# A linear recurrence and a soft mixture of experts on one core: wider slot-sum matmuls, and unread matmuls put at other places

## The chip, the cores and the metric

The kernel runs on one core of a Trainium2 chip. The metric is the device time of one execution in microseconds. Before the change it is 197.21 us, the median of three runs (196.96 to 197.81).

## The reference

Two layers, one after the other. The first is a gated recurrence over 5056 steps for 4 batches and 256 channels; the second is a soft mixture of 8 experts with 4 slots each, over all 20224 tokens.

```python
sig = 1.0 / (1.0 + np.exp(-f_logit))
f = lower_bound[None, None, :] + (1.0 - lower_bound[None, None, :]) * sig
i = 1.0 - f
for t in range(S):
    h = f[:, t] * h + i[:, t] * x[:, t]
    y[:, t] = h
...
logits = x @ phi                     # x is y, with batch and step as one axis
d = softmax(logits, over tokens)
slot_input = d.T @ x                 # 32 slots x 256
for e in range(E):                   # w1: 256 x 1024, w2: 1024 x 256 for each expert
    slot_out[e] = np.maximum(slot_input[e] @ w1[e], 0.0) @ w2[e]
c = softmax(logits, over slots)
out = c @ slot_out
```

## The kernel before, in words

The sequence is cut into groups of 512 steps (ten groups, the last one overlapping), and a unit is one group of one batch: 40 units, n = 0 to 39. SP's queue issues all loads of f_logit and x, in the order of the units, into three buffers each (`load`), so a load waits until an older buffer is free. Each unit then goes through a chain of engines, and the order of all instructions is written out by hand in the loop over n:

- `gate` (ACT) makes s_t, the sigmoid of minus f, two units at once; `enter` (POOL) multiplies it by x into u_t (unit 0 on DVE).
- `s_to_channels` and `u_to_channels` (TensorE) transpose s and u, so that channels lie on partitions. From unit 4 on u is transposed by `half_to_channels`, 64 rows at a time.
- `decay` (ACT) makes the decay factors a from the transposed s, and `scan` (DVE) runs the recurrence, two scans a unit.
- `to_tokens` (TensorE) transposes the result back into hp, and `keep_tokens` (DVE or ACT in turn) copies it to ht.
- `logits`, `exps` and `weights_to_tokens` make exp(logits) for a pair of groups in the order of slots (etall) and of tokens (et). `slots` adds up et.T @ ht in slot_ps: a matmul for each batch and each r of a group, with 32 columns of weights and 256 columns moving. Batch b's sums stand in partitions 32b and up, all in the first half of the bank slot_bank.

`idle` issues matmuls that nobody reads, into the second half of slot_bank, each with a 128x128 float32 operand held (ident_f) and 256 columns moving; the profile has two records for each. `spin` issues such matmuls in bfloat16 during the experts.

POOL also issues the weight loads (`load_w`): w1 of eight experts, then w2 of eight, three early ones at n = 9, 17 and 25 and the rest at n = 31 to 36, after the `enter` of that step. They convert float32 to bfloat16. The last two experts' w2 go to w_t, a reused f_t buffer, and the eighth expert's comes in three pieces.

After the last unit, the slot sums are copied to slot_sb by DVE, transposed into sin_ps (which lies in the bank `tail` together with the row sums), scaled to sin, and go through w1 (hi), a transpose, and w2: experts 0 to 3 into so4_ps, experts 4 to 7 into so_ps, one after the other (j = 0 to 3, eight matmuls each, line 696). DVE scales so_ps to slot_out. Only then the output can be made: matmuls of etall with slot_out (line 727) or slot_bd (lines 760 and 801), a scaling by DVE or ACT, and 20.7 MB of stores by SP. In the experts' stretch TensorE runs its instructions strictly in the order written.

Of the kernel before, what the change touches and what calls it, by code (L numbers as in the profile page):

```python
# [18 lines left out]
def kernel(  # L19
# [10 lines left out]
    nc = tc.nc  # L30
# [131 lines left out]
    with tc.tile_pool(name="sp2", bufs=3) as sp2, \  # L162
# [9 lines left out]
        slot_bank = pslot.tile([P, 2, D], F32, name="slot_ps")  # L172
        slot_ps = slot_bank[:, 0]

        wide_rep = rep.rearrange("p b s -> p (b s)").unsqueeze(1).broadcast_to([P, 2, P])

        def idle(k, first=False):
            if first:
                for i in range(2):
                    nc.tensor.matmul(slot_bank[:, 1, ds(0, P)], ident, ident,  # L180
                                     start=True, stop=False, skip_group_check=True)
            for _ in range(k):
                nc.tensor.matmul(slot_bank[:, 1], ident_f, wide_rep,  # L183
                                 start=False, stop=False, skip_group_check=True)
        xs, fs, sts, uts, pss, psus, hs, hps, hts, lgs, ets = ({} for _ in range(11))
# [73 lines left out]

        def half_to_channels(n, ps, t):  # L260
            k = ds(n % 2 * (P // 2), P // 2)
            v = ps.rearrange("c p r -> c (p r)").rearrange("c (p r) -> c p r", r=2 * R)
            for r in range(2 * R):
                nc.tensor.transpose(v[:, :, r], t(r)[k].bitcast(F32), ident_f[k, k])  # L264

# [9 lines left out]
        def u_to_channels(n):  # L275
            ps = psu.tile([P, P, R], F32, name="up", tag="up")
            if long(n):
                half_to_channels(n, ps, lambda r: uts[n - n % 2 + r // R][:, r % R])
# [139 lines left out]
        def left_over():  # L418
            for b in range(B):
                k = ds(b * NS, NS)  # L420
                nc.gpsimd.tensor_copy(left[k, :, b % 2], etall[k, ds(S - L, L)])

        def slots(g):
            n_p = rows(g)
            et, ht = ets.pop(g), hts.pop(g)
            for r in range(R):
                for b in range(B):
                    nc.tensor.matmul(slot_ps[ds(b * NS, NS), :], et[:n_p, r, b],
                                     ht[:n_p, b, r],
                                     start=(g == 0 and r == 0),  # L430
                                     stop=(g == n_grp - 1 and r == R - 1),
                                     skip_group_check=True)

# [36 lines left out]
        def late_slots():  # L470
            for r in range(R):
                for b in range(B):
                    nc.tensor.matmul(slot_ps[ds(b * NS, NS), :], ets[last][:, r, b],
                                     hts[last][:, b, r],
                                     start=False, stop=r == R - 1,
                                     skip_group_check=True)
# [6 lines left out]
        load(SINGLE)  # L483
        lb_constants()
        gate(0, 1)
        enter(0)
        s_to_channels(0)
        decay(0, 1, [0])
        u_to_channels(0)
        gate(1, 1)  # L490
        decay(0, 1, [1])
        phi_constants()
        enter(1)
        s_to_channels(1)
        u_to_channels(1)
        gate(2, 1)
        decay(1, 1)
        enter(2)
        for n in range(n_unit):
            if n < SINGLE - 2:  # L500
# [7 lines left out]
                if n + 3 == SINGLE:  # L508
                    gate(n + 3)
                if n % 2 == 0:  # L510
                    unit(load, n + AHEAD)
                unit(enter, n + 3)
                for b in range(2 * n, 2 * n + 2):
                    rep_constants(b)
            else:
                end = n >= n_unit - 6
# [30 lines left out]
                if n == n_unit - 2:  # L547
                    keep_tokens(n - 1)
                if n % 2 == 0:
                    unit(s_to_channels, n + 2)  # L550
                    unit(s_to_channels, n + 3)
                if n not in (n_unit - 3, n_unit - 2):
                    unit(u_to_channels, n + 1)
                if n in (n_unit - 5, n_unit - 4):
                    idle(2)
                elif n == SINGLE - 2:
                    idle(1, True)
                elif 2 * B <= n < n_unit - 4 and n % (2 * B) in (1, 5, 6, 7):
# [55 lines left out]
        slot_sb = slot_sb.rearrange("p t o -> p (t o)").bitcast(F32)[:, ds(0, D)]  # L614
        nc.vector.tensor_copy(slot_sb, slot_ps)
        sin_ps = tail[:, 0, ds(G // 2, DC * NS)].rearrange("p (o s) -> p o s", o=DC)
        slot_v = slot_sb.rearrange("p (c o) -> p o c", o=DC)
# [6 lines left out]
    with tc.tile_pool(name="ew", bufs=1) as ew, \  # L624
# [68 lines left out]
        nc.vector.reciprocal(rrow[:, :wide_r], rs_ps[:, :wide_r])  # L693
        for j in range(Q):
            for fc in range(FC):
                nc.tensor.matmul(so_ps, wide[:, fc, j].rearrange("p b s -> p (b s)"),
# [11 lines left out]
        nc.vector.tensor_scalar_mul(slot_out, so_ps, rcs)  # L708
# [161 lines left out]
```

## Time and profile before

| what | us |
|---|---|
| median of three runs | 197.21 |
| the profiled execution, whole | 197.01 |
| its span, first to last instruction | 195.2 |
| busy: TensorE, DVE, ACT, POOL | 150.6, 142.0, 138.8, 103.1 |
| first load issued; first f_t used by ACT | 0.72; 4.39 |
| first scan starts; last scan ends | 7.84; 125.6 |
| last weight issue; last weights landed | 126.92; 141.5 |
| first store issued | 143.58 |
| last instruction of the output stage on DVE and ACT | about 176.5 |

The scans of unit 0 start at 7.84 and those of unit 39 end at 125.6; in 110 to 120 us DVE is busy 10.00 of 10 us. Loads of x and f run until about 107 us, the weights until 141.5, the stores from 144 until about 193. The granted clock of TensorE is 0.50 in three stretches of 3.41 us, from 18.52, 35.59 and 49.24, and from 144.8 to the end; elsewhere the records show 1.00, and for the time before 15 us there is no record of it.

An idle time in a row, [0.27 <-DMA w_t], is the time the engine stood before the row's first instruction, with what ended it. PEld is the load of the held operand, PE the matmul itself; loads run ahead of matmuls.

### The profile page before, as it was taken

To read this page: it belongs to the slowest core of one execution; us is meant where nothing else is said; L and a number is where in the kernel's file an instruction comes from. 1 tells how busy PE (TensorE), PEld (TensorE's weight loads), DVE (VectorE), ACT (ScalarE), POOL (GpSimd) and SP (SyncE) were. 2 spreads that over 40 slices of the span, in tenths; PEclk is the share of its full clock that TensorE was granted. 3 is DMA by queue.
4 is the path that set the end of the run, shared out by engine and by line. 5 is a ranking of instruction groups with operands and counts; after the bars stand their busy time and mean duration, and the time that the engine had idled before them with its cause. 6 is when DMAs were issued, how large, how long until landed. Compare 5 with 4: busy or idle time off the path is not lost.

```text
span 195.2 us, 3283 instructions
## 1 busy us (share of the span) xinstructions
PE 150.6 (77%) x1222; PEld 108.7 (56%) x1222; DVE 142.0 (73%) x175; ACT 138.8 (71%) x192; POOL 103.1 (53%) x78
## 2 busy tenths in 40 slices
PE   0684896898998979989798976999997999980000
PEld 0474775765786657857576755766872663420000
DVE  2666699799699999999999999824288867770000
ACT  3686778599988998989988698724068788991000
POOL 2584888756798949776888979592030000000000
PEclk9998799699699999999999999999985555555555
DMA  6999999999999999999999999999949999999995
GB/s 203 415 433 428 426 425 421 430 426 411 326 428 426 423 334 405 423 425 414 324 418 418 235 212 214 214 212 211 170 165 428 425 431 426 430 433 430 430 430 218
DMA packets 12145, 70.75 MB, mean 362 GB/s; under 512 B 1361, under 2 KB 1874, under 8 KB 7650
## 3 DMA queue, kind: packets, MB, share of 16 engines
q1 hardware_dynamic: 9504, 62.13, 76.3%
q0 software_dynamic: 2624, 8.42, 21.8%
q8 instruction: 9, 0.15, 0.3%
q14 instruction: 6, 0.05, 0.1%
q10 hardware_dynamic: 2, 0.00, 0.0%
HBM read 58.23 MB, written 20.71 MB: 404 GB/s over the span
## 4 chain that ended last, share of the span: by engine, by line
PE 36%; DVE 28%; DMA 17%; ACT 4%; issue 4%; SPq 1%; POOL 0%; ACTq 0%
DVE h L332 17%; DMA w_t<-in_moe_w_dram 7%; PE op L801 7%; PE sp L249 7%; PE op L727 6%; DMA w_sb<-in_moe_w_dram 6%; PE hp L345 5%; DVE ht L364 5%; PE up L264 4%; DMA f_t<-in_f_logit_dram 4%; DVE h L319 3%; DVE oc L717 2%; PE op L760 2%; ACT s_t L234 1%; PE lg L378 1%
## 5 line engine op out<-in xcount | busy, mean ns | idle before, releaser
L245 POOL TENSOR_TENSOR u_t<-s_t,x_t 128x1024 bf16<-128x1024 bf16 (+1 forms) x39 | 82.4, 2129 | 24.5 <-ACT s_t L234 14.2
L332 DVE TENSOR_TENSOR_SCAN h<-a,h,up 128x512 bf16<-128x512 f32 x64 | 78.1, 1267 | 9.0 <-PE up L264 4.3
L234 ACT ACTIVATE s_t<-f_t 128x2048 bf16<-128x2048 f32 (+2 forms) x22 | 38.1, 1736 | 2.9 <-DMA f_t<-in_f_logit_dram 2.9
L345 PE MATMUL hp<-ident_f,h 128*128 128x128 f32 (+1 forms) x160 | 29.3, 307 | 8.4 <-DVE ht L364 6.3
L297 ACT ACTIVATE a<-sp,lbs 128x1024 f32<-128x1024 bf16 x28 | 29.6, 1112 | 4.6 <-PE sp L249 4.5
L345 PEld LDWEIGHTS hp<-ident_f,h 128*128 128x128 f32 (+1 forms) x160 | 23.2, 206 | 17.0 <-DVE ht L364 11.5
L249 PE MATMUL sp<-ident_f,s_t 128*128 128x128 f32 x144 | 23.7, 315 | 7.0 <-ACT s_t L234 5.7
L249 PEld LDWEIGHTS sp<-ident_f,s_t 128*128 128x128 f32 x144 | 19.6, 164 | 8.7 <-ACT s_t L234 6.5
L264 PE MATMUL up<-ident_f,u_t 64*128 64x64 f32 x224 | 21.4, 236 | 2.4 <-POOL u_t L245 2.4
L264 PEld LDWEIGHTS up<-ident_f,u_t 64*128 64x128 f32 x224 | 17.0, 144 | 7.1 <-POOL u_t L245 2.8
L721 ACT ACTIVATE ob<-op,rrow 128x256 f32<-128x256 f32 x32 | 12.4, 478 | 9.1 <-PE op L727 8.7
L364 ACT COPY ht<-hp 128x512 f32<-128x512 f32 (+1 forms) x21 | 12.2, 583 | 7.9 <-PE hp L345 7.9
L304 ACT ACTIVATE a<-sp,lbs 128x512 f32<-128x512 bf16 (+2 forms) x16 | 13.2, 868 | 2.9 <-PE sp L249 2.7
L183 PE MATMUL slot_ps<-rep,ident_f 128*128 128x256 f32 x42 | 14.2, 426 | 0.0
L364 DVE COPY ht<-hp 128x512 f32<-128x512 f32 (+1 forms) x19 | 12.7, 668 | 1.0 <-PE hp L345 1.0
L801 PE MATMUL op<-slot_bd,etall 64*128 64x512 bf16 x32 | 13.1, 627 | 0.0
L812 ACT ACTIVATE oc<-op,rrow 128x256 f32<-128x256 f32 x32 | 12.2, 486 | 0.8 <-PE op L801 0.3
L727 PE MATMUL op<-slot_out,etall 32*128 32x256 bf16 x64 | 12.6, 375 | 0.1
L806 DVE TENSOR_TENSOR oc<-op,rrow 128x1024 f32<-128x1024 f32 x8 | 9.7, 1223 | 3.4 <-PE op L801 3.4
L717 DVE TENSOR_TENSOR ob<-op,rrow 128x1024 f32<-128x1024 f32 (+2 forms) x12 | 9.8, 862 | 2.2 <-DMA out_dram<-ob 1.1
L727 PEld LDWEIGHTS <-etall 32*128 32x128 bf16 x64 | 8.9, 153 | 3.8 <-issue 1.3
L378 PE MATMUL lg<-h,phi 128*32 128x512 bf16 (+1 forms) x80 | 9.9, 389 | 0.2 <-ACT et L402 0.2
(109 smaller groups left out, 168.9 us busy)
## 6 DMA issues: line engine op xcount, KB each, us to landing
f_t<-in_f_logit_dram SPq DMA_DIRECT2D x14, 1024.0 KB, 11.2
x_t<-in_x_dram SPq DMA_DIRECT2D x14, 1024.0 KB, 9.5
out_dram<-oc SPq DMA_DIRECT2D x4, 2048.0 KB, 13.1
w_sb<-in_moe_w_dram POOLq DMA_DIRECT2D x14, 512.0 KB, 9.5
out_dram<-ob SPq DMA_DIRECT2D x3, 2048.0 KB, 9.6
f_t<-in_f_logit_dram SPq DMA_DIRECT2D x8, 512.0 KB, 7.0
x_t<-in_x_dram SPq DMA_DIRECT2D x8, 512.0 KB, 6.1
out_dram<-oc SPq DMA_DIRECT2D x4, 896.0 KB, 6.0
```

The lines of the kernel that those rows point to most:

```text
L183: nc.tensor.matmul(slot_bank[:, 1], ident_f, wide_rep, start=False, stop=False, skip_group_check=True)
L234: nc.scalar.activation(s_t, f_t, ACT.Sigmoid, scale=-1.0)
L245: nc.gpsimd.tensor_tensor(uts[n][:, :r], s_t[:, :r], x_t[:, :r], ALU.mult)
L249: nc.tensor.transpose(ps[:, :, r], t[:, r].bitcast(F32), ident_f)
L264: nc.tensor.transpose(v[:, :, r], t(r)[k].bitcast(F32), ident_f[k, k])
L297: nc.scalar.activation(a, sp[:, :, :, :, o], ACT.Identity, scale=nomlb[:, ds(o, 1)], bias=1.0)
L332: nc.vector.tensor_tensor_scan(h[:, :T, o], decays[n // 2, o][:, n % 2, :T], up[:, :T, o], hs[number(g - 1, b)][:, ds(used(g - 1) - 1, 1), ...
L345: nc.tensor.transpose(hp[:n_p, r], hw[:, :n_p, r], ident_f)
L364: copy(hts[g][:n_p, b].rearrange("p r d -> p (r d)").bitcast(F32), hps.pop(n)[:n_p].rearrange("p r c -> p (r c)"))
L717: nc.vector.tensor_tensor(ob, op, scale.broadcast_to(list(ob.shape)), ALU.mult)
L727: nc.tensor.matmul(op[:, j], ew[:, :, r + j], slot_out[ds(b * NS, NS)], start=True, stop=True, skip_group_check=True)
L801: nc.tensor.matmul(op[:, i_r].rearrange("p u d -> p (u d)"), ew[:, :, r + i_r], slot_bd[ds(j * 2 * NS, 2 * NS)].rearrange("s u d -> s (u d)"),
```

## The change

- `idle` no longer holds ident_f but zeros: the tile `left`, cleared at the start and filled only at the end, read as 64 float32 columns. So it adds zero to the sums of batches 0 and 1, and holds 64 columns in place of 128. What moves is ident_f repeated (`plain`) or rep.
- There are 36 such matmuls in place of 21: ten among units 0 to 3, one each at n = 2, 3, 5 and 7, and two within the transposes of unit 12; 20 stay where they were. The two bfloat16 ones that opened the bank go.
- The gate of units 4 and 5 is issued as two halves, and POOL's last two rep constants come before `enter` of unit 4, not after.
- `slots` of groups 0 to 5 takes two batches in one matmul: 64 columns of weights, 512 columns moving, 8 matmuls a group in place of 16. Only the blocks of a batch with itself are read, so sums of odd batches now stand in the second half of the bank (`slot_of`). The other groups still take 16.
- The slot sums are copied in four pieces, two by DVE and two by ACT, and sin_ps gets a bank of its own.
- Six spins of 512 columns stand before expert 6 (j == 2), and two of 512 behind the last expert in place of eight of 128.

```diff
-        slot_ps = slot_bank[:, 0]
+        zeros = left.rearrange("s t u -> s (t u)").bitcast(F32)
...
-        def idle(k, first=False):
-            if first:
-                for i in range(2):
-                    nc.tensor.matmul(slot_bank[:, 1, ds(0, P)], ident, ident,
-                                     start=True, stop=False, skip_group_check=True)
-            for _ in range(k):
-                nc.tensor.matmul(slot_bank[:, 1], ident_f, wide_rep,
-                                 start=False, stop=False, skip_group_check=True)
+        plain = ident_f.unsqueeze(1).broadcast_to([P, 2, P])
+
+        def idle(k, first=False, moving=wide_rep):
+            for i in range(k):
+                nc.tensor.matmul(slot_bank[ds(0, L), 0], zeros, moving,
+                                 start=first and i == 0, stop=False, skip_group_check=True)
...
-        def half_to_channels(n, ps, t):
+        def half_to_channels(n, ps, t, rests=False):
...
             for r in range(2 * R):
+                if r == R and rests:
+                    idle(2)
...
+        PAIRED = 6
+
+        def slot_of(b):
+            return slot_bank[ds(b * NS, NS), b % 2]
+
         def slots(g):
...
             for r in range(R):
+                if g < PAIRED:
+                    for b in range(0, B, 2):
+                        nc.tensor.matmul(slot_bank[ds(b * NS, 2 * NS)],
+                                         et[:n_p, r, ds(b, 2)].rearrange("p b s -> p (b s)"),
+                                         ht[:n_p, ds(b, 2), r],
+                                         start=(g == 0 and r == 0), stop=False,
+                                         skip_group_check=True)
+                    continue
                 for b in range(B):
-                    nc.tensor.matmul(slot_ps[ds(b * NS, NS), :], et[:n_p, r, b],
-                                     ht[:n_p, b, r],
-                                     start=(g == 0 and r == 0),
-                                     stop=(g == n_grp - 1 and r == R - 1),
-                                     skip_group_check=True)
+                    nc.tensor.matmul(slot_of(b), et[:n_p, r, b], ht[:n_p, b, r],
+                                     start=False, stop=False, skip_group_check=True)
...
         lb_constants()
+        idle(3, True, plain)
         gate(0, 1)
...
         u_to_channels(0)
+        idle(2, moving=plain)
         gate(1, 1)
...
         s_to_channels(1)
+        idle(1, moving=plain)
         u_to_channels(1)
...
                 if n + 3 == SINGLE:
-                    gate(n + 3)
+                    gate(n + 3, 1)
+                    gate(n + 4, 1)
                 if n % 2 == 0:
                     unit(load, n + AHEAD)
-                unit(enter, n + 3)
+                if n == 0:
+                    unit(enter, n + 3)
                 for b in range(2 * n, 2 * n + 2):
                     rep_constants(b)
+                if n:
+                    unit(enter, n + 3)
...
+                if n == SINGLE - 2:
+                    idle(4, moving=plain)
                 if n % 2 == 0:
                     unit(s_to_channels, n + 2)
...
-                elif n == SINGLE - 2:
-                    idle(1, True)
+                elif n in (SINGLE - 2, SINGLE - 1, SINGLE + 1, SINGLE + 3):
+                    idle(1)
...
-        nc.vector.tensor_copy(slot_sb, slot_ps)
-        sin_ps = tail[:, 0, ds(G // 2, DC * NS)].rearrange("p (o s) -> p o s", o=DC)
+        for b in range(B):
+            copy = nc.scalar.copy if b % 2 else nc.vector.tensor_copy
+            copy(slot_sb[ds(b * NS, NS)], slot_of(b))
+        sin_ps = psu.tile([P, DC, NS], F32, name="sin_ps", tag="up")
...
         for j in range(Q):
+            if j == 2:
+                spin(tail[:, 1], 6, G)
             for fc in range(FC):
...
-        spin(tail[:, 1], 8, P)
+        spin(tail[:, 1], 2, G)
```

More of the change, by code (lines that the diff above doesn't have):

```diff
@@ L277, in u_to_channels @@
             if long(n):
-                half_to_channels(n, ps, lambda r: uts[n - n % 2 + r // R][:, r % R])
+                half_to_channels(n, ps, lambda r: uts[n - n % 2 + r // R][:, r % R],
+                                 n == 3 * B)
             elif n // B == odd:
@@ L472, in late_slots @@
                 for b in range(B):
-                    nc.tensor.matmul(slot_ps[ds(b * NS, NS), :], ets[last][:, r, b],
+                    nc.tensor.matmul(slot_of(b), ets[last][:, r, b],
                                      hts[last][:, b, r],
```

## The prediction

> **What bounds the kernel now.** I read the slices of the page first, because they show which resource has no holes.
>
> ```profile
> PEclk9998799699699999999999999999985555555555
> DMA  6999999999999999999999999999949999999995
> GB/s 203 415 433 428 426 425 421 430 426 411 326 428 426 423 334 405 423 425 414 324 418 418 235 212 214 214 212 211 170 165 428 425 431 426 430 433 430 430 430 218
> HBM read 58.23 MB, written 20.71 MB: 404 GB/s over the span
> ```
>
> Every engine has slices of 8 or less; the DMA row has only 9s between its first slice and slice 30. The 212 GB/s of slices 23 to 28 is no slack: weights are read as float32 and stored as bfloat16, so 212 moved is 424 read. Next, stretches of 2 us around the one hole (columns: stretch, length, busy PE, PEld, DVE, ACT, POOL, then clock, DMA share, GB/s):
>
> ```profile
> 138.00:140.00 2.00, 2.00 (x23) 1.78 (x22) 0.76 (x2) 0.00 (x0) 0.00 (x0) 1.00 1.09 191
> 140.00:142.00 2.00, 1.73 (x18) 1.32 (x17) 0.02 (x1) 0.00 (x0) 0.00 (x0) 1.00 0.45 76
> 142.00:144.00 2.00, 1.87 (x21) 1.70 (x19) 1.58 (x5) 0.96 (x3) 1.36 (x2) 1.00 0.00 0
> 144.00:146.00 2.00, 1.96 (x10) 1.11 (x10) 2.00 (x4) 2.00 (x7) 0.47 (x1) 0.70 0.82 313
> ```
>
> Then the chain that ended last, where it crosses that hole:
>
> ```profile
> 115.00 11.64 DMA w_sb<-in_moe_w_dram
> 126.64 0.28 issue
> 126.92 14.59 DMA w_t<-in_moe_w_dram
> 141.52 0.04 issue
> 141.56 0.39 PE so_ps L696 x2
> 141.95 0.02 issue
> 141.98 0.49 DVE slot_out L708
> ```
>
> So the span of 195.2 is: about 2.6 us until the reads run at full rate; reads of 58.23 MB until the last weights land at 141.5 (419 GB/s over these 139 us); about 2.9 us without DMA while the last two expert matmuls, slot_out and the first output rows are made; 20.71 MB of writes until the DMA share falls at about 192.8 (428 GB/s); and some 2.4 us of closing. The profiled execution took 197.01, 1.81 more than its span; the median of the runs shown is 197.21 (196.96 to 197.81), so it stands 0.2 under the median.
>
> No byte, no DMA issue and no order within SP's queue changes. The change can move the end only through the hole: by when the last weights land, or by when TensorE has done the last expert.
>
> **How much room TensorE has there.** The timeline of TensorE and of its loads at the hole:
>
> ```profile
> 139.50 1.79 PE L696 MATMUL so_ps<-w_t,wide 128*128 128x256 bf16 x14
> 141.56 0.38 PE L696 MATMUL so_ps<-w_t,wide 128*128 128x256 bf16 x2 [0.27 <-DMA w_t<-in_moe_w_dram]
> 141.56 0.10 PEld L696 LDWEIGHTS <-wide 128*128 128x128 bf16 x1 [0.44 <-issue]
> ```
>
> The load for the last two matmuls stood 0.44 us: TensorE is only 0.44 us ahead of the last weights. Work put before that point costs what exceeds 0.44, unless TensorE arrives earlier. Call X the time by which it reaches j == 2 (139.50) earlier than before.
>
> **The parts.**
>
> Unread matmuls before the seventh expert (j == 2): six of 512 columns. None of that size at full clock is in the trace. Fourteen of 256 columns start over 1.79 less one of 0.27, 0.117 each, so 512 would take 0.23; by the old spins (eight of 128 columns in 0.61, 0.076 each) 0.30. At half clock, 32 op matmuls of 512 columns (L801) took 13.07, 0.41 each. Bounds 1.3 to 2.5 for six; I take 1.4, since the clock is 1.00 there. The delay of the last expert is then 1.4 - 0.44 - X, or 0.96 - X, never below nothing. The two spins left behind the experts (0.47) take the place of 0.61 and run beside slot_out's 0.49: nothing; uncovered, 0.47.
>
> Slot sums copied in four pieces, and sin_ps in a bank of its own: one DVE copy (0.42) becomes two on DVE and two on ACT, each priced by the whole copy or by ACT's 0.48 for 256 columns, so +0.42 to +0.54. Against it, DVE's sin waited 1.49 for row sums of the same bank, ending 131.21 though the sums' transposes were done at 130.46; that wait goes. The row sums stay in TensorE's queue ahead of the experts, so they begin about where they did: 0 (-0.5 to +0.3).
>
> First units. The largest idle time of DVE in the scans is here, and two more follow:
>
> ```profile
> 21.44 2.46 DVE L332 TENSOR_TENSOR_SCAN h<-a,h,up 128x512 bf16<-128x512 f32 x2 [2.63 <-PE up L249]
> 39.11 2.45 DVE L332 TENSOR_TENSOR_SCAN h<-a,h,up 128x512 bf16<-128x512 f32 x2 [1.51 <-PE up L264]
> 52.80 2.45 DVE L332 TENSOR_TENSOR_SCAN h<-a,h,up 128x512 bf16<-128x512 f32 x2 [1.61 <-PE up L264]
> ```
>
> All three stand behind TensorE at half clock (0.50 in 18.52 to 21.94, 35.59 to 39.00 and 49.24 to 52.66). At 21.44 the path was: gate of two units (1.91, to 18.47), eight transposes in 1.97, four in 0.8. Split, the first gate ends near 17.6, the second near 18.7 (1.06 each); at full clock the last four transposes of s take 0.63 and u's 0.63, so the scan starts near 20.05: +1.4 (0.5 to 1.8; the four unread matmuls end before 18.6 and so hold s back by up to 1 us). Rep constants moved past enter on POOL, two of 0.31, cost nothing: POOL would wait for the gate there anyway. The gap at 52.80 is met by two unread matmuls and by heavier slot sums in the stretch before it: +1.6 (0 to 1.6). The one at 39.11 gets one or two more matmuls in a stretch with 1.85 of 3.41 us busy: +0.5 (0 to 1.5). In the very first units three unread matmuls start after lb_ps at 3.55; at the half clock by which an old pair took 0.91 (21.47) they end near 6.2, and s_t is ready at 5.50; if they bring the clock up by 8.3 it is won back: 0 (-1.3 to +0.6).
>
> Slot sums of six groups: 16 matmuls of 32x256 took 0.62; now 8 of 64x512. The nearest row is the logits, 8 of 512 columns at two places of the array in turn, 1.08. So +0.46 a group, 2.8 us of TensorE in all (0 to 7.3, by 8 x 0.23 each). Half of it hides beside the scans; where DVE waits for u (0.39 at 55.64, 0.38 at 101.07) it shows. I take -1.0 (0 to -2.8).
>
> Unread matmuls of half the columns, 20 of them at the old places: their effect on the clock. I compared windows of 3.41 us that ended in a drop with those that didn't:
>
> ```profile
> 45.83:49.24 3.41, 2.44 (x30) 1.62 (x30) 3.41 (x5) 3.38 (x3) 1.22 (x1) 1.00 1.03 390
> 69.72:73.14 3.42, 2.45 (x30) 1.65 (x30) 3.42 (x5) 3.42 (x4) 2.26 (x2) 1.00 1.04 313
> 103.86:107.27 3.41, 2.59 (x19) 1.88 (x18) 3.41 (x5) 2.82 (x3) 3.39 (x3) 1.00 1.03 422
> 152.00:174.00 22.00, 22.00 (x76) 11.46 (x75) 16.90 (x15) 19.29 (x51) 0.00 (x0) 0.50 1.02 429
> ```
>
> The first dropped, the next two didn't, at equal busy time; and 22 us of full busy time with 32 or 64 rows stayed at half clock. Weighting each matmul's streaming time by its rows times columns over 128x128, I get 0.40, 0.41 and 0.41 for the first three: the clock seems to follow how much of the array is used, with a threshold near 0.4. By that estimate a half-wide unread matmul counts half, and 103.86 would fall to about 0.35. One such late drop costs DVE what the old ones did, about 1.5. I take half a drop: -0.8 (0 to -3). The Trainium skill, "TensorE: Matmul & The Clock Gate" ("The HAM clock gate"), says that the clock falls after an idle window of some 3.4 us. The trace agrees with the 3.41 us steps, but not that the window must be idle: 45.83 to 49.24 was 2.44 busy. By the skill's rule the narrower matmuls would cost nothing and X would be 0.8 larger.
>
> Sum: X = 1.4 + 1.6 + 0.5 + 0 - 1.0 - 0.8 + 0 = 1.7. That is above 0.96, so TensorE reaches the last weights before they land (141.5), and the hole is as before. What X exceeds 0.96 by is lost in waiting for weights: they can't land earlier, as the DMA share before them is 0.98 or more. So 197.01 + 0, or 197.2 against the median; I write 197.1.
>
> **Rivals.**
>
> 1. Slower: TensorE late at the seventh expert. If the clock drops after about 57 us (two or three drops at 1.5) or the slot sums cost 2.8, X is -0.5 to -1.5, and the six unread matmuls, which no wait hides any more, push the last expert by 0.96 + 0.5 to 1.5: 198.5 to 199.5. It decides from X = 0, where the time is 198.0. For it: scans keep DVE busy 10.0 of 10 us from 110 on, so nothing is won back there. Against it: DVE was idle 9 us in its first 50.
>
> 2. Faster: an earlier start fills the queues better and the last weights land sooner. From 140.00 to 141.25 the DMA share fell from 0.99 to 0.35; filled, that saves 0.4, and issues of POOL no longer held by a late scan might save as much again: 196.2. Against it: the last issues waited for earlier weight DMAs, not for POOL's work.
>
> 3. The change doesn't keep the clock up in the first units (half-wide again): X about -1, the same path as rival 1, with DVE's three gaps still there: 199.0.
>
> **Numbers.** No change to the end 0.70, rival 1 and 3 together 0.19, rival 2 0.11. A difference of 0.5% is 0.99 us, about what a measurement of this kernel can tell. The forecast's own range is 196.5 to 198.0 (X from 0 up, and the spread of runs); the low end stretches to 196.3 for rival 2 and the high end to 198.5 for the near part of rival 1. Rivals 1 and 3 make up slower, rival 2 faster.
>
> **What would show it.** Right: the last w_t lands at 141.5 within 0.5, the two last so_ps matmuls still start on that landing, DVE ends its scans 1 to 3 us before 125.6, no DVE wait over 1.5 in 18 to 54. Wrong: spins that end after w_t has landed, half-clock windows between 57 and 125, or a DMA share under 0.9 before 140. If weights land before 140.5, the claim that DMA bounds the first part is false.

## The result, and the profile after

The change made the kernel slower: 199.56 us, the median of six runs (199.16 to 200.78), against 197.23 for six runs of the kernel before (196.96 to 197.81). The ratio is 1.0127, with an interval of 1.0106 to 1.0149. The forecast of no change, 197.1 within 196.5 to 198.0, was wrong. The profiled execution took 199.62, its span is 197.8 (195.2 before). Runs of one kernel differ in their mean granted clock (0.857 to 0.879 in these six), and a ratio leaves out runs far above the fastest, so a median and a ratio need not agree.

The slices of the page after:

```profile
PEclk9999879999999999999999999999999555555555
DMA  5999999999999999999999999999529999999995
GB/s 209 418 432 427 427 421 427 429 426 381 356 426 421 414 328 429 421 430 368 363 417 381 203 210 214 215 212 211 97 108 433 422 421 444 444 434 424 424 424 215
HBM read 58.23 MB, written 20.71 MB: 399 GB/s over the span
```

The clock row has one dent where it had three. The unread matmuls help, but not in every execution alike: up to the first slot sums at 47 us the runs e1, e3, e6, e7, e8 and e10 below have the same instructions, and at half clock they spend there two, no, two, one, two and one steps of 3.41 us (two to four in the kernel before and its variants e4, e5, e9, e13 and e14). The bytes are the same. But the one hole of the DMA row, a 4 in one slice before, is now a 5 and a 2. The same stretches of 2 us as before (stretch, length, busy PE, PEld, DVE, ACT, POOL, then clock, DMA share, GB/s):

```profile
140.00:142.00 2.00, 1.95 (x13) 1.16 (x12) 0.71 (x2) 0.00 (x0) 0.00 (x0) 1.00 0.55 85
142.00:144.00 2.00, 2.00 (x18) 1.66 (x17) 0.00 (x0) 0.00 (x0) 0.00 (x0) 1.00 0.01 2
144.00:146.00 2.00, 1.85 (x15) 1.46 (x14) 1.58 (x5) 0.94 (x3) 1.34 (x2) 1.00 0.04 8
146.00:148.00 2.00, 1.96 (x12) 1.16 (x11) 2.00 (x4) 2.00 (x7) 0.49 (x1) 1.00 0.51 188
```

The DMAs stand still from 142 to 146, twice as long as before, and TensorE is busy all that time. The chain of waits names the work:

```profile
129.82 0.42 DVE slot_sb L637
130.24 0.02 issue
130.26 0.37 ACT slot_sb L637
130.64 0.02 issue
130.66 0.43 DVE slot_sb L637
131.09 0.02 issue
131.12 0.37 ACT slot_sb L637
...
139.91 0.89 PE so_ps L720 x8
140.81 0.33 PE tail L152
141.14 0.05 issue
141.19 1.02 PE tail L152 x4
142.22 1.76 PE so_ps L720 x16
143.98 0.02 issue
144.00 0.50 DVE slot_out L732
```

Where a DMA of w_t stood before, there is now an unbroken chain of TensorE's own work: TensorE reaches j == 2 at 140.81 (139.50 before), spins for 1.41 and runs the last 16 matmuls without a wait. They end at 143.98 (141.95), and the first store is issued at 145.61 (143.58): 2.03 later. The four copies stand in the chain one behind the other, 1.67 us from 129.82 to 131.49; one copy of 0.42 stood there before.

The other 0.57 lies behind the first store. From its issue to the last packet of the stores it takes 50.54 us, 49.97 before. What differs is seen among the packets of the trace, not among the instructions. The page's third part counts them on a queue of their own (packets, MB, share):

```profile
q8 instruction: 9, 0.15, 0.3%
```

These are 16 KB packets that fetch instructions, mostly 0.9 to 1.0 us each, on average one for every 250 of TensorE's records (100 to 330 in these two executions), and the page before has the same line. That they belong to TensorE is seen below, where added matmuls bring a tenth. What matters is the place of the ninth: 141.2 before, in the hole, and 145.6 now, at the issue of the first store, where it took 1.27 us and the second store's issue took 1.17 us in place of 0.38.

This table, from the packets and the instructions of each profiled execution, is used from here on (us; "records" are TensorE's matmul and load records):

```
run                               records  last fetches          last w_t  1st store  store stage  span
before                               2480  135.3  141.2            141.18     143.58       49.97  195.2
after                                2439  139.1  145.6            142.33     145.61       50.54  197.8
e1_no_spins_at_j2                    2440  140.5  147.4            144.56     146.93       50.71  199.3
e2_two_copies                        2448  138.8  147.1            144.67     147.00       50.75  199.4
e3_single_batch_sums                 2536  130.3  138.7  169.2     142.10     144.44       51.05  197.1
e4_spins_alone                       2480  134.8  140.9            141.06     143.95       49.97  195.6
e5_small_ones_before                 2536  131.5  139.3  169.1     142.04     144.39       51.00  197.0
e6_small_ones_after                  2479  137.7  143.0            143.30     146.70       49.96  198.3
e7_small_and_no_spins                2480  136.2  142.0            141.93     144.31       49.97  195.9
e8_two_groups_single                 2471  139.6  143.9            143.78     146.21       49.96  197.8
e9_weights_earlier                   2480  139.9  143.7            143.54     145.93       49.97  197.6
e10_first_units_only                 2536  131.5  138.6  169.3     142.22     144.62       50.90  197.1
e11_first_units_fewer_instructions   2464  133.1  142.7            141.21     143.59       49.96  195.2
e12_spins_with_early_scans           2463  137.8  142.0            141.23     144.45       49.96  196.1
e13_small_ones_at_the_end            2536  135.4  142.5  179.3     142.47     144.80       51.01  197.4
e14_eight_at_the_start               2496  133.5  141.2            141.51     143.86       49.96  195.5
```

"Last w_t" is the end of the last packet of the weights; the semaphore that TensorE waits for comes some 0.3 later, at the 141.5 of the table of before. "1st store" is its issue. First store, store stage and some 1.65 of closing make up the span of every row. In the three runs whose ninth fetch falls on the first stores (after, e1, e2) the second store's issue took 1.17, 1.35 and 1.38, and the store stage is 50.54 to 50.75.

### The profile page after: what moved, and what is told of

Same layout as the page of the kernel before. It is cut to its first block, busy times and chain, and to the rows that moved or that the text cites. A ratio compares the mean times of both kernels' runs of the same rounds, so it can differ in the third digit from the quotient of the medians.

```text
span 197.8 us, 3246 instructions
## 1 busy us (share of the span) xinstructions
PE 156.9 (79%) x1201; PEld 105.2 (53%) x1202; DVE 142.5 (72%) x176; ACT 139.7 (71%) x195; POOL 103.0 (52%) x78
## 4 chain that ended last, share of the span: by engine, by line
PE 34%; DVE 23%; ACT 12%; DMA 12%; POOL 4%; issue 4%; SPq 1%; ACTq 0%; POOLq 0%; DVEq 0%
DVE h L333 13%; DMA x_t<-in_x_dram 9%; PE op L825 7%; PE hp L346 5%; PE up L264 4%; POOL u_t L243 4%; PE sp L247 4%; DVE h L320 4%; DMA out_dram<-ob 3%; DVE ht L365 3%; ACT oc L791 2%; PE lg L379 2%; ACT s_t L232 2%; PE so_ps L720 2%; ACT a L298 2%
## 5 line engine op out<-in xcount | busy, mean ns | idle before, releaser
L346 PE MATMUL hp<-ident_f,h 128*128 128x128 f32 (+1 forms) x160 | 29.8, 310 | 6.0 <-DVE ht L365 4.4
L346 PEld LDWEIGHTS hp<-ident_f,h 128*128 128x128 f32 (+1 forms) x160 | 22.3, 207 | 19.4 <-DVE ht L365 10.2
L247 PE MATMUL sp<-ident_f,s_t 128*128 128x128 f32 x144 | 20.9, 288 | 3.0 <-ACT a L305 1.6
L264 PE MATMUL up<-ident_f,u_t 64*128 64x64 f32 x224 | 20.8, 231 | 3.0 <-POOL u_t L243 2.9
L264 PEld LDWEIGHTS up<-ident_f,u_t 64*128 64x128 f32 x224 | 16.5, 140 | 7.9 <-POOL u_t L243 4.0
L247 PEld LDWEIGHTS sp<-ident_f,s_t 128*128 128x128 f32 x144 | 17.2, 149 | 5.7 <-ACT s_t L232 3.2
L181 PE MATMUL slot_ps<-rep,left 128*64 128x256 f32 x52 | 16.0, 398 | 0.0
L333 DVE TENSOR_TENSOR_SCAN h<-a,up 128x512 bf16<-128x512 f32 x8 | 9.4, 1211 | 1.5 <-PE up L264 0.8
```

Source lines behind the costliest of these rows:

```text
L181: nc.tensor.matmul(slot_bank[ds(0, L), 0], zeros, moving, start=first and i == 0, stop=False, skip_group_check=True)
L247: nc.tensor.transpose(ps[:, :, r], t[:, r].bitcast(F32), ident_f)
L333: nc.vector.tensor_tensor_scan(h[:, :T, o], decays[n // 2, o][:, n % 2, :T], up[:, :T, o], hs[number(g - 1, b)][:, ds(used(g - 1) - 1, 1), ...
L346: nc.tensor.transpose(hp[:n_p, r], hw[:, :n_p, r], ident_f)
```

## The experiments

### What the six spins cost

Spins added to the kernel before, at the same place (two of 512 in place of eight of 128 at the end, as in the change):

```diff
         for j in range(Q):
+            if j == 2:
+                spin(tail[:, 1], 6, G)
```

> The kernel before with only the six unread matmuls of 512 columns before the seventh expert, and two of 512 behind the last in place of eight of 128. Theory: TensorE is 0.44 us ahead of the last weights there and six cost 1.41 (the changed profile), so the last expert is 0.97 late: 197.23 -> 198.2. Rival (the last weights land later anyway in most executions, so the room is 1 us or more): 197.2 to 197.5.

Measured: 197.63 (196.98 to 200.3, ten runs), ratio 1.0018 [0.9991, 1.0046]. The first store came 0.37 later, less than expected, because in this run TensorE reached j == 2 0.35 earlier than in the run before.

The reverse, the changed kernel with the spins taken out and the old eight put back:

```diff
-            if j == 2:
-                spin(tail[:, 1], 6, G)
...
-        spin(tail[:, 1], 2, G)
+        spin(tail[:, 1], 8, P)
```

> The changed kernel without the six unread matmuls before the seventh expert; the eight of 128 columns stand behind the last expert again. Theory (the last expert is late, its parts add up): the six took from 140.81 to 142.22 in the changed profile. Without them the 16 matmuls would end near 142.6, or near 142.75 if they must wait for weights that landed at about 142.4, against 143.98: 1.2 to 1.4 us off, 199.56 -> 198.2 to 198.4. Rival (the late weights and the long second store issue, 1.17 against 0.38, set the end by themselves): nothing to 0.5 us off, 199.1 to 199.6.

Measured: 200.31 (198.12 to 201.81, ten runs), ratio 1.0105 [1.0052, 1.0158]. A clear miss: no gain. (Its fastest run, 198.12, lies close to the theory's 198.2, but has no trace.) In its profile two stretches at half clock fell among the first units, and the scans ended at 127.7, two late against before. TensorE was no longer last; the weights were:

```profile
142.70 1.96 PE L718 MATMUL so_ps<-w_t,wide 128*128 128x256 bf16 x14 [0.37 <-DMA w_t<-in_moe_w_dram]
144.91 0.38 PE L718 MATMUL so_ps<-w_t,wide 128*128 128x256 bf16 x2 [0.25 <-DMA w_t<-in_moe_w_dram]
```

They landed 3.4 later than before, in part because the DMAs ran short in a stretch that I had called saturated. The kernel without spins first, then the kernel before, in the same two microseconds:

```profile
108.00:109.00 1.00, 0.60 (x4) 0.56 (x4) 1.00 (x3) 0.56 (x1) 1.00 (x1) 1.00 1.49 336
109.00:110.00 1.00, 1.00 (x19) 0.93 (x18) 1.00 (x3) 0.59 (x1) 1.00 (x2) 1.00 0.57 135
```

```profile
108.00:109.00 1.00, 1.00 (x15) 0.68 (x15) 1.00 (x3) 0.83 (x1) 0.67 (x2) 1.00 1.06 270
109.00:110.00 1.00, 1.00 (x13) 0.52 (x9) 1.00 (x3) 1.00 (x2) 1.00 (x1) 1.00 1.20 225
```

In the second of them the DMA share is 0.57 against 1.20, though some of that is only moved from the first (1.49 against 1.06). The first weights of n = 31 were issued at 107.35 there and at 105.46 before: POOL issues them behind `enter`, and loads of x and f wait for the buffers that `enter` frees. By 108 us 0.30 MB less had been read than before, by 118 us 0.75 MB (from the packets, weights counted as float32); at the 424 GB/s of these stretches that is 1.8 us. Three more runs with late scans (e2, e6, e8) are 0.45 to 0.62 MB behind at 118 us. So late scans do reach the reads, through the buffers.

### Where the fetch falls

20 small unread matmuls (32 columns held, 2 moving) in TensorE's wait for the copies of the changed kernel, which bring the ninth fetch forward into the hole:

```diff
+        def small(dst, k):
+            for _ in range(k):
+                nc.tensor.matmul(dst, ident[:, :NS], ident[:, :2],
+                                 start=True, stop=True, skip_group_check=True)
...
         row_sums(0, range(10))
+        small(tail[:NS, 1, :2], 20)
```

> The changed kernel with 20 more unread matmuls of 32x2, while TensorE waits for the copies of the slot sums (130.5 to 131.5): its instruction count is that of the kernel before. Theory (fetches): the fetch at 145.6, which held up the second store issue for 1.17 us, moves back into the hole; the last expert is as late as before. The stores run 0.6 shorter: 199.56 -> 199.0, and the second store issue takes about 0.4. Rival (the store issue is slow for another reason, such as the full clock of TensorE there): 199.4 to 199.9.

Measured: 199.0 (197.78 to 200.55, ten runs), ratio 1.0082 [1.0039, 1.0126]. The store stage is 49.96, as before the change, and the second store's issue was normal again. The profiled execution is not a typical one of its runs (200.13; scans end at 127.2).

The same with the spins out as well:

> The changed kernel with 20 small unread matmuls in the wait for the copies (these put the ninth instruction fetch back into the stretch without DMA, as with e6) and without the six spins before expert 6. Theory (paired slot sums on the path of DVE, four copies in a chain, a fetch in the stores and the spins each have a share): the first store no longer waits for the spins, and the store stage is 49.96, but the last scan is still late and the reads behind it too, so 198.2 to 199.2. Rival (the spins are the loss, and the fetch only blurred it in e1): 197.5 or less. Rival (without spins TensorE waits for weights instead, as in e1): the same as e6, 199.0 to 199.6, with the last w_t at 144 or later.

Measured: 198.68 (197.5 to 201.41, twelve runs; six of them from 197.50 to 197.75), ratio 1.0057 [1.0019, 1.0094]. This profile is the best counterpart of the changed kernel's: its scans end at 126.0 (126.1), the stretch at half clock is 23.6 to 27.0 (23.7 to 27.1). Its first store is 1.30 earlier and its store stage 0.57 shorter, and its span 1.9 less. The second rival's landing of 144 did not come: 141.93.

28 of the small matmuls at the start of the kernel before, where TensorE is idle:

```diff
         lb_constants()
+        small(slot_bank[:NS, 1, :2], 28)
         gate(0, 1)
```

> The kernel before with 28 more unread matmuls of 32x2 at the start, while TensorE waits for the first s_t (3.55 to 5.50), and nothing else. They put TensorE's instruction count to that of e3 (56 more). Theory (instruction fetches: packets of 16 KB on queue q8 that come with every 256 or so instructions of TensorE and hold a DMA engine for 0.9 to 1.3 us): the fetch that stood at 141.2, in the hole without DMA, comes before the last weights (near 139) and a tenth one falls among the stores, as in e3 (138.7 and 169.2); the last weights land 0.9 later and the stores end 1.0 later: 197.2 -> 198.6 to 199.1. Rival (the time of e3 came from its clock, its copies or its unread matmuls): 197.0 to 197.5.

Measured: 198.94 (nine of ten runs from 198.74 to 198.99), ratio 1.0064 [1.003, 1.0098]. The scans ended earlier than before (124.8), and still 56 instructions without any task cost 1.8 us. The table shows two halves: the ninth fetch came ahead of the last weights and these landed 0.86 later; a tenth fell into the stores, and their stage took 1.03 more. To part the place of a fetch from the number of instructions, 28 small ones behind the last matmul of the output, and then only 8 at the start:

> The kernel before with 28 small unread matmuls (32x2) behind the last matmul of the output, about 176 us, where TensorE has nothing else to do; the first nine fetches stay where they are. Theory (a fetch occupies one DMA engine and costs what it takes when that engine is the last): a tenth fetch near 170 to 177, nothing else changed: last w_t at 141.2, first store at 143.6, store stage 50.9 to 51.1 in place of 49.97, so 198.0 to 198.4. Rival (in e5, e3 and e10 the loss comes from work on TensorE or from places before the hole, not from the fetch): 197.0 to 197.4.

Measured: 198.27 (197.68 to 201.06, twelve runs), ratio 1.0036 [1.001, 1.0062]; the medians differ by 1.01. The tenth fetch came at 179.3, long after everything else that the edit touches, and the store stage is 51.01. The stretches of half a microsecond at the end show what it does to the stores, first of this kernel, then of the kernel before:

```profile
194.00:194.50 0.50, 0.00 (x0) 0.00 (x0) 0.00 (x0) 0.00 (x0) 0.00 (x0) 0.50 0.09 33
194.50:195.00 0.50, 0.00 (x0) 0.00 (x0) 0.00 (x0) 0.00 (x0) 0.00 (x0) 0.50 0.08 33
195.00:195.50 0.50, 0.00 (x0) 0.00 (x0) 0.00 (x0) 0.00 (x0) 0.00 (x0) 0.50 0.08 33
```

```profile
192.50:193.00 0.50, 0.00 (x0) 0.00 (x0) 0.00 (x0) 0.00 (x0) 0.00 (x0) 0.50 0.17 66
193.00:193.50 0.50, 0.00 (x0) 0.00 (x0) 0.00 (x0) 0.00 (x0) 0.00 (x0) 0.50 0.00 0
```

For the last 1.5 us a share of 0.08 is left, about one DMA engine of 16 (1/16 is 0.06), and 33 GB/s over half a microsecond is one 16 KB packet: the other engines have finished, one is behind. Which engine served the fetch the trace doesn't tell. In this execution the weights also landed 1.3 late, with the scans as before (125.6); it took 199.22, 0.95 above the median of its runs, and why is open.

> The kernel before with 8 of those small matmuls at the start (28 in e5): the ninth fetch comes about 0.5 us earlier, near 140.6, ahead of the last w_t packets, and there is no tenth. Theory (it is the place of the fetch that costs): last w_t at 141.6 to 142.1, store stage 49.97, 197.7 to 198.2, or no change if the fetch comes at 141.0 or later. Rival (the number of instructions at the start costs in proportion, 8/28 of the 1.8 of e5): 197.7 with w_t at 141.2 and a longer store stage.

Measured: 197.3 (196.99 to 198.44, twelve runs), ratio 0.999 [0.9966, 1.0014]. The ninth fetch stayed at 141.2 and there is no tenth; the median did not change (in the profile the last weights landed 0.33 later). So the cost doesn't grow with the number of instructions, but comes with the place of a fetch. The Trainium skill, "Runtime: NRT & Kernel Launch" ("Instruction fetch mechanics"), says that instructions come in blocks of 16 KiB, 256 at a time, and that the cost of crossing into the next block is "mostly hidden". The packets agree with the size; that it is hidden holds for e14 and for the hole of the kernel before, not for e5 (1.8 us) or e13 (1.0 us), where the DMAs are the bound.

### The slot sums and their copies

Two copies in place of four, of one half of the bank by DVE and of the other by ACT, meant to run at once, with the unread blocks masked in the transposes:

```diff
-        for b in range(B):
-            copy = nc.scalar.copy if b % 2 else nc.vector.tensor_copy
-            copy(slot_sb[ds(b * NS, NS)], slot_of(b))
+        nc.vector.tensor_copy(slot_sb[:, ds(0, D)], slot_bank[:, 0])
+        nc.scalar.copy(slot_sb[:, ds(D, D)], slot_bank[:, 1])
...
+            for u in range(2):
+                nc.tensor.matmul(sin_ps[:, o], slot_v[:, u, o], sides[:, u],
+                                 start=u == 0, stop=u == 1, skip_group_check=True)
```

> The changed kernel with the slot sums copied in two pieces, a half of the bank by DVE and one by ACT, at the same time; the blocks that aren't wanted are multiplied by zero in the transposes, eight of them for four. Theory: four copies in a chain took 129.82 to 131.49, 1.67 us; two side by side take about 0.5, the added transposes about 0.3, so the experts start 0.8 to 0.9 earlier and nothing hides it: 198.7. Rival (the six unread matmuls or late weights hide it): 199.3 to 199.6.

Measured: 199.35 (198.99 to 201.19, four runs), ratio 1.0112 [1.0028, 1.0196]. TensorE reached j == 2 at 140.3, half a microsecond earlier than in the changed kernel with the scans ending at nearly the same time (126.3), but in the profiled execution the weights landed at 144.67, so the gain shows in no time. Nor did the copies run at once: DVE's starts at 129.95 and takes 0.42, ACT's waits for it and starts at 130.41. A miss, and no test of copies side by side. All these copies read one bank, slot_bank; whether that is why they wait for each other was not tested.

All slot sums one batch at a time again (PAIRED = 0, and the flag that starts the sums set for the first group):

> The changed kernel with one batch in each slot-sum matmul for all groups (the sums of odd batches stay in the second half of the bank, the four copies stay). Theory: DVE's waits of 0.92 and 0.24 behind each pair of groups shrink to about 0.39, 2.3 us in all; the scans end near 124 and the last expert is limited by the landing of the weights: 1.2 to 2.0 us off, 197.6 to 198.4. Rival (the narrow unread matmuls, not the slot sums, hold u back, or lighter sums let the clock fall and give it back): 199.0 to 199.6, with stretches of clock 0.50 after 57 us.

Measured: 198.98 (198.71 to 199.91, ten runs), ratio 1.0077 [1.0044, 1.0109]. The scans end at 123.6, 2.5 earlier, yet the span is only 0.8 shorter: its 97 records more bring the ninth fetch to 138.7 and a tenth to 169.2, like e5. The miss led to e5.

Two groups of the six single again (PAIRED = 4):

> The changed kernel with the slot sums of four groups, not six, by two batches in a matmul: 32 more instructions of TensorE. Theory (fetches): the count is eight under that of the kernel before, so no fetch falls between 139.5 and the hole's end but in it, and none among the stores; with a third of the pairs' cost gone (0.8 of 2.3), the last expert is 0.8 earlier: 198.0 to 198.5, lower than both the changed kernel (199.56) and e3 (198.98). Rival (TensorE's time alone): between the two, near 199.3.

Measured: 199.19 (197.76 to 201.22, ten runs), ratio 1.0067 [1.0021, 1.0113]. The fetch is in the hole and the store stage 49.96 as expected, but two stretches at half clock fell among the first units, and the scans ended at 126.7: the median missed.

### The first units without the rest

The changed kernel with single-batch sums in one half of the bank, one DVE copy, no spins at j == 2:

```diff
-        PAIRED = 6
+        PAIRED = 0
...
-            return slot_bank[ds(b * NS, NS), b % 2]
+            return slot_bank[ds(b * NS, NS), 0]
...
+        nc.vector.tensor_copy(slot_sb, slot_bank[:, 0])
...
+        spin(tail[:, 1], 8, P)
```

> The changed kernel with single-batch slot sums in one half of the bank, one DVE copy, and no spins at j == 2 (eight short ones at the end again): what is left is the first units, the narrow unread matmuls, the split gate and the bank for sin_ps. Theory: scans end near 123.6, no expert is late, but the instruction count is like e3's, so a fetch falls before 140 and one into the stores (near 169): 198.0 to 198.9. Rival (instruction count doesn't matter): 197.2 or less. Rival (narrow unread matmuls themselves lose the clock): scans end after 125.6.

Measured: 198.99 (198.88 to 200.08, eight runs), ratio 1.009 [1.0059, 1.0121]. As the theory had it, 1.7 lost to two fetches, though the scans end at 124.7 (1.0 early) and TensorE waits for the seventh expert's weights:

```profile
137.04 1.03 PE L716 MATMUL so_ps<-w_sb,wide 128*128 128x256 bf16 x8
140.71 1.69 PE L716 MATMUL so_ps<-w_t,wide 128*128 128x256 bf16 x14 [2.64 <-DMA w_t<-in_moe_w_dram]
```

This run has the same stretch at half clock as the changed kernel (23.5 to 26.9), so the two tell what the paired sums cost. The three waits of DVE that differ most in the later scans, first of the changed kernel, then of this one:

```profile
54.45 2.46 DVE L333 TENSOR_TENSOR_SCAN h<-a,h,up 128x512 bf16<-128x512 f32 x2 [0.92 <-PE up L264]
...
77.85 2.46 DVE L333 TENSOR_TENSOR_SCAN h<-a,h,up 128x512 bf16<-128x512 f32 x2 [0.92 <-PE up L264]
...
101.27 4.97 DVE L333 TENSOR_TENSOR_SCAN h<-a,h,up 128x512 bf16<-128x512 f32 x4 [0.93 <-PE up L264]
```

```profile
54.04 2.45 DVE L333 TENSOR_TENSOR_SCAN h<-a,h,up 128x512 bf16<-128x512 f32 x2 [0.76 <-PE up L264]
...
76.91 2.45 DVE L333 TENSOR_TENSOR_SCAN h<-a,h,up 128x512 bf16<-128x512 f32 x2 [0.39 <-PE up L264]
...
99.79 4.97 DVE L333 TENSOR_TENSOR_SCAN h<-a,h,up 128x512 bf16<-128x512 f32 x4 [0.39 <-PE up L264]
```

Each time it waits for the transposes of u, which stand in TensorE's queue behind the slot sums: 1.23 more in these three waits. The scans end 1.49 later (126.15 against 124.66), but 0.25 of that was there before the first slot sums at 47.0 (the scan at 30.44 here starts at 30.19 there), so the paired sums cost 1.23.

The same with every unread matmul of the recurrence in bfloat16, 512 columns in one pass, so that there are 72 records fewer; and that once more with the spins at j == 2:

> As the kernel before this one, with each unread matmul of the recurrence in bfloat16, 64x512 in one pass, in place of 64x256 float32 in two, so 36 or more instructions fewer. Theory: scans end 1 to 2 us before 125.6 as in e3, and if the ninth fetch falls between 140.5 and 143.5 the time is that of the kernel before, 196.9 to 197.5, about 1 less than the run above. Rival (an earlier chain is worth time): 196.3 or less. Rival (first units cost something by themselves): 198 or more though the ninth fetch is in the stretch without DMA.

> As the kernel before this one, with the six spins of 512 columns before expert 6 and two at the end. Theory (the last expert is late by 0.96 - X and X is about +2 here): no delay, the same as the run above within 0.3. Rival (spins cost 1.0 to 1.4 wherever TensorE stands): 198.2 or more, with the first store 1 us later.

The first: 197.71 (196.8 to 202.45, twelve runs), ratio 1.0005 [0.9974, 1.0037]. The ninth fetch is in the hole, and though TensorE had done the sixth expert nearly two us earlier than before, the profiled span is 195.2, the same. Its chain of waits is the old one, nearly to the hundredth:

```profile
126.96 14.56 DMA w_t<-in_moe_w_dram
141.52 0.04 issue
141.56 0.39 PE so_ps L716 x2
141.96 0.02 issue
141.98 0.49 DVE slot_out L728
```

Against e10 it is 1.3 less (median; 1.9 by span) with scans that end within 0.7 of each other.

The second: 200.5 (196.79 to 203.48, twelve runs), ratio 1.0005 [0.9956, 1.0053]. Here the scans were not early: the clock stood at half from 103.9 to 114.2, and they ended at 126.3. TensorE reached j == 2 at 139.65, 0.15 late, and the first store came 0.87 later than before. Two of its runs (196.79 and 197.04) lie where the runs without spins do; that the spins were hidden in those two is likely, but they have no trace. Neither kernel beats the one before.

### Weights issued earlier

The kernel before with the weights of `load_w` moved to earlier steps:

```diff
-W_AT = {9: 1, 17: 1, 25: 1, 31: 1, 32: 1, 33: 2, 34: 3, 36: 6}
+W_AT = {9: 1, 17: 1, 25: 1, 29: 1, 31: 2, 32: 2, 33: 2, 34: 4, 36: 2}
```

> The kernel before with weights issued earlier: one at n = 29, two at 31, 32 and 33, four at 34 and two at 36, for one, one, two, three and six at 31, 32, 33, 34 and 36. Theory (from 108 on POOL's issues leave the DMA queue short: 180 to 209 GB/s of 217 in 110 to 117): up to 0.35 us of reading is won: 196.8. Rival (the queue was full enough; TensorE is only 0.44 ahead and earlier weights delay the last x, so the last expert waits for TensorE): 197.1 to 197.6.

Measured: 197.2 (196.97 to 199.98, ten runs), ratio 0.999 [0.9948, 1.0032]. No gain: the time is the rival's. Its profiled execution is far above the median (199.34, scans to 127.8), so its trace doesn't show why.

## Why the prediction was wrong, by its steps

**Right: what decides.** TensorE at the seventh expert, against the last weights, decides the end, and the first rival named the path and the sign. Six spins were put at 1.4 and took 1.41. The delay of the last expert was to be 0.96 - X, from 1.4 less a lead of 0.44. The lead was larger: j == 2 to the end took 2.45 before (139.50 to 141.95) and takes 1.76 without a wait, so 0.69; the wait shown in the trace was not all of it, the 14 matmuls ahead of it also ran slower (1.79, against 1.76 for all 16). With 0.72 - X in place of 0.96 - X the five runs with spins whose chain of waits goes through them come out to the hundredth (j == 2 is the first spin of that chain):

```
run      j == 2 at    X       0.72 - X   first store later by
e4         139.15    +0.35      0.37            0.37
e12        139.65    -0.15      0.87            0.87
after      140.81    -1.31      2.03            2.03
e8         141.41    -1.91      2.63            2.63
e6         141.90    -2.40      3.12            3.12
```

And where X was large (e11, about +1.9), it was lost waiting for weights, as the forecast had it for 1.7.

**Wrong: X.** It was put at +1.7 and was -1.31. How far the scans are ahead of the kernel before tells where it went (us, at the scans that start there at these times):

```
run     24.39   26.83   52.80   95.80   end of scans
after    1.06   -0.67    1.73    0.34   -0.52
e10      1.31   -0.42    1.98    1.28    0.97
e3       1.10    0.84    3.02    2.34    2.03
```

- First units, +3.5 together (1.4, 1.6, 0.5, 0): the step that failed most. The three waits shown in the prediction shrank as said: 2.63 to 0.99, 1.61 to 0.33, and 1.51 to none, and where the clock stayed up (e3) the lead at 52.80 is 3.0. By the end of the scans the changed kernel had only some 0.7 of it. But the changed kernel's clock fell once too, at 23.7 to 27.1, in a stretch for which no term was put, and DVE waited 0.77 and 1.83 there:

```profile
23.70:27.10 3.40, 3.40 (x19) 3.04 (x19) 1.96 (x2) 1.08 (x2) 3.40 (x2) 0.50 1.01 424
```

```profile
27.49 2.46 DVE L333 TENSOR_TENSOR_SCAN h<-a,h,up 128x512 bf16<-128x512 f32 x2 [1.83 <-PE up L264]
```

  In the 3.41 us before that stretch TensorE was busy for 1.77, as it waited 1.64 for POOL's u_t. In e3 the steps of 3.41 us fall elsewhere on the same instructions (18.8 to 22.2 with 2.27 busy, 22.2 to 25.6 with 2.91), and the clock stayed up. So 1.0 to 1.3 of the lead at 52.80 hangs on the execution. Rival 3 had named this failure, with X about -1, but with the three old gaps still there, which they were not. Another 1.0 goes from 52.80 to the end in e3 and e10, which have no paired sums; why is open.
- Paired slot sums, -1.0: near right. They cost 1.23 (after against e10). Each group took the 1.05 to 1.08 that the logits row gave. That is 0.43 more in the first group of a pair and 0.53 in the second (logits and sums 1.99 from 50.97, 1.46 from 52.69 before), 2.9 in all. Half hides, as said: the 0.53 is what DVE's wait for u grew by (0.39 to 0.92).
- Late drops of the clock, -0.8: none in the changed kernel (one to 27.1, then none until 153.4), none before the stores in e10 or e3. The rule of weighted rows and columns predicted a drop that did not come: by the same weighting (an estimate) the window from 105.6 to 109.0 of the changed kernel comes to 0.35, and the clock stayed up. With one-pass bfloat16 matmuls drops did come (e11 at 70.2, e12 at 103.9).
- Copies, 0 (-0.5 to +0.3): they cost 0.6. This step counted two copies for each engine side by side. They run in turn, each waiting for the other engine's, 1.25 longer than the one copy. From the end of the scans to the end of the sixth expert it takes 14.04 in the kernel before, e4, e5, e13 and e14, 14.65 to 14.68 in the six profiles with four copies, and 13.37 to 13.62 with one copy and a bank of its own for sin_ps (e10, e11, e12). So the four copies cost 1.0 to 1.3, and the wait for row sums that went was worth 0.4 to 0.7.

Summed: 1.73 - 1.0 - 1.23 - 0.6 is -1.1; the last 0.16 is in how X is read, as 139.50 is the start of the first matmul at j == 2, and 140.81 the end of the one ahead of it (139.66 before).

**Missing: the fetches.** "No byte, no DMA issue and no order within SP's queue changes" was true of the program's own transfers, and the conclusion, that only the hole can move the end, was false. The ninth fetch, pushed from the hole into the first stores, cost 0.57.

**Wrong as a rule: late scans cost only through TensorE.** "They can't land earlier" held (e9, e11), but they can land later: e1. In the changed kernel itself the last weights landed 1.15 later than before, hidden behind the spins; with the spins out (e7) their landing set the end, 0.73 after the old one.

So the 2.6 us of span are: 0.57 for the fetch, 1.30 that go when the spins go too (e7), and 0.73 that stay, TensorE and the weights both being late then. Of the 2.03 before the first store, 1.31 is TensorE's lateness and 0.72 spins, as the table has it; the two splits differ because without spins the weights are next.

Open: why the weights landed 0.75 to 1.15 later in e7 and in the changed kernel, whose DMA share in 108 to 114 us is about 1.0 or more as before (their last issues waited for older weights, and were 0.2 and 1.2 later), and 1.3 later in e13. In all three, and in e3, e5 and e10, the packets of the last half microsecond before the landing come one at a time, where half a microsecond before its landing the kernel before has a dozen at once: one DMA engine is behind the others, as at the end of the stores of e13. The changed kernel has a fetch at 139.1, as e3, e5 and e10 have at 138.6 to 139.3, which may be what put it behind; e7 and e13 have none there. Open too is what starts the stretches at half clock, which fall at other times in each profile and probably spread the medians of e1, e2, e8 and e12.

## What to carry to other kernels

When DMA sets the end, price work by where it stands against the last landing, and fill a wait only as far as every run, not the best one, has it. Count what an edit does to the number of instructions on the busiest queue: the instruction fetches go through the same DMAs, and the one that falls into a stall is free while the one that falls into the stores is not. Split copies of one small tile over two engines only if the trace shows them side by side: here neither four nor two were.

## Unexpected of the hardware

- 28 tiny matmuls (56 records) in an idle stretch of TensorE cost 1.8 us of 197 (e5), 28 more behind all other matmuls 1.0 (e13), and 8 at the start nothing (e14): a fetch packet occupies DMA for 0.9 to 1.4 us, and one late engine is waited for.
- A store's issue at the time of a fetch took 1.17 us in place of 0.38 (1.35 and 1.38 in e1 and e2).
- A single-pass bfloat16 matmul of 512 columns kept the clock up less well than two passes of float32 with 256, as far as two profiles tell (drops at 70.2 and 103.9 in e11 and e12; none between 57 and 140 in the profiles with float32).
